# Third-stage operands split from the transposition's bank, weight preparation and activations re-ranked, six first weight loads issued by GpSimd: a fused chunk attention and two-stage mixture kernel

## The chip, the core and the metric

The kernel runs on one core of one Trainium2 chip. The metric is the device time of one execution in microseconds (us). The median of three executions of the kernel before is 812.74 us (812.33 to 813.37). The trace comes from another execution, recorded by the hardware profiler: it took 814.69 us, of which 812.9 us lie between the first and the last instruction (the span). What is worked out from the trace is compared with 814.69 and then taken over to the median, which is 1.95 us lower.

## The reference

Three stages follow each other; every one takes the result of the one before.

```
attention: per chunk of 32 queries, keys = 8 memory keys + 16 left + 32 own + 8 right (W = 64)
    a = exp(q k^T / sqrt(64) - max);  a = a / (sum(a) + 1e-9);  out = a @ v        (2 x 8 heads x 768 x 64)
x  = out as [1536 tokens, 512]
moe:   p = probs / (sum(probs) + 1e-9);  x = sum over 4 experts of p[e] * (relu(x @ w1[e]) @ w2[e])   (512 -> 1024 -> 512)
moe2:  h = x @ w_in;  g = h if h > 0 else exp(min(h, 0)) - 1;  out = g @ w_out       (512 -> 2048 -> 512)
```

All is computed to float32 accuracy. TensorE gets it by three products of two parts: a value is split into a rounded high part (a cast on ScalarE) and the rest (a subtraction on VectorE or GpSimd), and each product is high x high + low x high + high x low.

## The kernel before, in words

The 1536 tokens are two halves g = 0, 1 of 768, each six blocks of 128. The hidden layers are cut into units u of 512 hidden values: eight in the mixture (4 experts x 2), four in moe2 (u = 8 to 11). A step of the program is a unit and a half; the sequence is (0,0), (1,0), (1,1), (2,1), (2,0), ..., (7,0), (7,1), (0,1), (8,0), (8,1), ..., (11,1), 24 steps.

Each step has an "up" part and a "down" part. Up multiplies tokens by w1 or w_in with seven block products instead of eight (a Strassen form). Its token operands are seven matrices of 128 x 768 per half: three are blocks of x (B11, B21, B22, numbered 0, 1, 2) and four are sums and differences of blocks (T1, T2, T3, T4N, numbered 3 to 6). They are called xh (high) and xl (low) with half and number: xl1_5 is the low part of operand 5 of half 1. The weights' parts are uh and ul. One step's up is 84 matmuls of 128x384 (L570; L630 in the first step). Down multiplies the activated hidden values (hh, hl, four row groups f of 128, two token halves) by w2 or w_out (dh, dl): 72 matmuls of 128x512 (L664).

The helper `split_task` adds the two tasks of every split: ScalarE's cast (L249) and the subtraction (L245) on VectorE or GpSimd. `combine` builds the seven operands of a half from the transposed x, which lies in the SBUF buffer `area`: it needs subtractions of blocks for the T operands, then seven splits. Before the third stage x is the sum y of the second; `flip` transposes it, one block of 128 tokens at a time, into PSUM bank 6 or 7 (L709), and ScalarE copies the bank to `area` (L712). `activate` turns a product into hh and hl: for moe2 two ScalarE functions (L519, L520), one VectorE operation (L525), a cast to hh (L530) and a subtraction to hl.

`load_pair` loads a unit's w1 (two tiles rawp, 512 KB each), `prep_down` its w2 (four tiles rawd, 256 KB each), and both split them. `block_at` adds the attention of a block; its key, query and value loads (L759, L765) go out on SyncE's DMA queue, as the weight loads do. `convert` puts w_in and w_out, which come with 64-bit words, into float32 and stores them in DRAM for the third stage.

The order on every engine is set by a small planner in the program. Every task has an engine, an estimated duration and a rank; the planner repeatedly picks, for the engine that is free first, the ready task of the lowest rank, and emits it. RANK and BY are tables of such ranks and of engine choices. The emitted order is then fixed: an engine works through its own list and stands still when the next entry isn't ready.

Of the kernel before, what the change touches and what calls it, by code (L numbers as in the profile page):

```python
# [19 lines left out]
P = 128  # L20
# [39 lines left out]

RANK = {
# [117 lines left out]
def kernel(ctx, tc, att, w1, w2, w_in, w_out, probs, out):  # L179
# [90 lines left out]
    def split_blocks(u, j, i, rank, o, n, to=0, by=None):  # L270
# [14 lines left out]
    def prep_pair(u, j, rank, lead, by=None, plain=False):  # L285
        load_pair(u, j, rank - lead)
# [124 lines left out]
    def combine(g, rank, late, spare, parts, engs):  # L411


        base, rest = combiner(g, spare, parts, engs)
        base(rank, late)
        rest(late)

    def combiner(g, spare, parts, engs):
# [10 lines left out]
        def split(o, b, rank, name=None):  # L429
            for i, c in enumerate(cut):  # L430
                eng = pick(f"b{g}{o if name is None else name}{i}", "V") if parts > 1 or spare else "V"
                split_task(
                    rank,
                    2 * n,
                    b[0][:, :, c],
                    keys(b, c),
                    lambda c=c: xh[g][o][:, :, c],
                    ("xh", g, o, i) if parts > 1 else ("xh", g, o),
                    lambda c=c: xl[g][o][:, :, c],
                    ("xl", g, o, i) if parts > 1 else ("xl", g, o),  # L440
                    eng,
                )
            if parts > 1:
                for k in ("xh", "xl"):
                    join[k, g, o] = [(k, g, o, i) for i in range(parts)]
# [14 lines left out]
        def base(rank, late, plain=False):  # L460
            split(B11, blk(0), rank)
            split(B21, blk(2), rank)
            if plain:
                split(B12, blk(1), late, 7)
                split(B22, blk(3), late)

        def rest(late, plain=False):
            if spare:
                s0 = 2 * KT * TN
                t2 = area[:, s0 : s0 + 2 * TN].rearrange("p (k t) -> p k t", k=2), [grains(s0, TN), grains(s0 + TN, TN)]  # L470
                diff(engs[0], blk(0), blk(1), blk(0), late)
                diff(engs[1], t2, blk(3), blk(0), late)
                diff(engs[2], blk(1), blk(3), blk(1), late)
            else:
                t2 = blk(3)
                diff(engs[0], blk(0), blk(1), blk(0), late)
                split(B22, blk(3), late)
                diff(engs[1], blk(1), blk(3), blk(1), late)
                diff(engs[2], t2, blk(3), blk(0), late)
            diff(engs[3], blk(2), blk(2), t2, late)  # L480
            split(T2, t2, late)
            split(T3, blk(1), late + 1)
            split(T4N, blk(2), late + 3)
            split(T1, blk(0), late + 5)
            if spare and not plain:
                split(B22, blk(3), late + 7)

        return base, rest
# [65 lines left out]
    def up(u, g, rank):  # L554
# [3 lines left out]
        for n, (p, j) in enumerate([(p, j) for j in range(2) for p in ORDER] if apart else [(p, j) for p in ORDER for j in range(2)]):  # L558
# [20 lines left out]
            add("PE", 1.051, r, mm, [("uh", j, i), ("ul", j, i)] + xkeys(g, ib), kb)  # L579
# [36 lines left out]
    def plain(half, rank):  # L616

        for n, (q, f) in enumerate([(q, f) for f0 in (0, 2) for q in range(2) for f in (f0, f0 + 1)]):
# [19 lines left out]
            add("PE", 1.051, rank + n, mm, [("uh", j, i), ("ul", j, i)] + xkeys(0, ib), kb)  # L638
# [62 lines left out]
    def flip(g, tb, rank):  # L701
# [9 lines left out]
        add("PE", 0.49, rank, turn, [("y", g, tb)], [("b", b)])  # L711
# [288 lines left out]
```

## Time and profile before

| what | value |
|---|---|
| median of 3 executions | 812.74 us (812.33 to 813.37) |
| profiled execution | 814.69 us |
| its span | 812.9 us |
| mean granted TensorE clock | 0.998 of full speed |
| busy TensorE / weight load / VectorE / ScalarE / GpSimd | 799.4 / 722.0 / 517.9 / 421.2 / 295.9 us |
| moved by DMA | 72.13 MB, mean 89 GB/s |

A busy time is the sum over an engine's instructions, and its share is of the span. TensorE is busy for 799.4 us of 812.9, so 13.5 us of the span are left in which it does nothing. A row of a timeline gives the start in us, the duration in us, the engine, the line, what is written and read, and how many like instructions stand in a row; a bracket behind it is idle time of the engine before it and what ended that. Matmuls overlap in the pipeline, so what one costs is the distance from its start to the next start, not its duration.

### The profile page before, as it was taken

How to read it: one execution, taken by the hardware profiler on the slowest of the kernel's cores; microseconds unless marked ns; L12 is line 12 of the kernel's file. 1: busy time of each engine (PE TensorE's matmuls, PEld its weight loads, DVE VectorE, ACT ScalarE, POOL GpSimd, SP SyncE). 2: the span in 40 equal slices, each digit the busy share in tenths (PEclk: the TensorE clock that was granted, in tenths of full speed). 3: DMA queues.
4: the chain of work that ended last, by engine and by line, in shares of the span. 5: the costliest groups of instructions: out<-in, count | busy, mean ns of one | idle time of the engine just before them, and what ended most of it. 6: DMA issues, size and time to landing. Idle time of an engine off the chain costs nothing.

```text
span 812.9 us, 12177 instructions
## 1 busy us (share of the span) xinstructions
PE 799.4 (98%) x4684; PEld 722.0 (89%) x4684; DVE 517.9 (64%) x832; ACT 421.2 (52%) x857; POOL 295.9 (36%) x266
## 2 busy tenths in 40 slices
PE   7999999999999999999999999999999999999998
PEld 6888889989989989989989989899798898998997
DVE  5895557986965976965865734855535537538534
ACT  5976636625525425425425436457566555555642
POOL 2547275215215214324323325754216216206202
PEclk9999999999999999999999999999999999999999
DMA  8974112722411521511421300212003003000012
GB/s 307 341 248 165 33 46 84 220 91 72 166 67 59 194 79 40 204 56 66 156 78 65 130 1 1 85 44 78 1 1 104 0 1 93 11 1 0 35 45 79
DMA packets 27419, 72.13 MB, mean 89 GB/s; under 512 B 3168, under 2 KB 3424, under 8 KB 27360
## 3 DMA queue, kind: packets, MB, share of 16 engines
q1 hardware_dynamic: 27360, 71.34, 26.0%
q8 instruction: 37, 0.61, 0.3%
q14 instruction: 22, 0.18, 0.1%
HBM read 59.79 MB, written 11.53 MB: 88 GB/s over the span
## 4 chain that ended last, share of the span: by engine, by line
PE 86%; ACT 3%; issue 3%; DMA 2%; DVE 2%; POOL 2%; SPq 0%; POOLq 0%; ACTq 0%
PE bank L664 46%; PE bank L570 36%; DMA qk<-in_att_dram 2%; PE bank L630 1%; POOL area L245 1%; PE bank L862 1%; POOL hl L245 1%; DVE xl L245 1%; ACT abd L850 1%; PE bank L785 1%; ACT xh L249 1%; ACT e L813 0%; ACT hh L500 0%; ACT hh L530 0%; PE bank L842 0%
## 5 line engine op out<-in xcount | busy, mean ns | idle before, releaser
L664 PE MATMUL bank<-dh,hl 128*128 128x512 f32 x580 | 226.0, 390 | 2.0 <-DVE hl L245 2.0
L664 PE MATMUL bank<-dh,hh 128*128 128x512 f32 x580 | 226.6, 391 | 0.1
L664 PE MATMUL bank<-dl,hh 128*128 128x512 f32 x580 | 225.7, 389 | 0.0
L570 PE MATMUL bank<-xh,uh 128*128 128x384 f32 x644 | 218.2, 339 | 0.4 <-ACT p L582 0.4
L570 PE MATMUL bank<-xh,ul 128*128 128x384 f32 x644 | 216.8, 337 | 0.0
L570 PE MATMUL bank<-xl,uh 128*128 128x384 f32 x644 | 216.8, 337 | 0.0
L245 POOL TENSOR_TENSOR hl<-c,hh 128x384 fp32r<-128x384 f32 x63 | 71.8, 1147 | 216.1 <-ACT hh L530 214.8
L664 PEld LDWEIGHTS bank<-dh,hl 128*128 128x128 f32 x580 | 109.3, 188 | 25.5 <-DVE hl L245 2.4
L664 PEld LDWEIGHTS bank<-dh,hh 128*128 128x128 f32 x580 | 109.3, 188 | 21.9 <-ACT hh L500 0.5
L664 PEld LDWEIGHTS bank<-dl,hh 128*128 128x128 f32 x580 | 109.4, 189 | 21.3
L570 PEld LDWEIGHTS bank<-xh,uh 128*128 128x128 f32 x644 | 120.9, 188 | 1.9 <-ACT p L582 0.7
L570 PEld LDWEIGHTS bank<-xl,uh 128*128 128x128 f32 x644 | 120.9, 188 | 0.9
L570 PEld LDWEIGHTS bank<-xh,ul 128*128 128x128 f32 x644 | 120.9, 188 | 0.0
L302 POOL TENSOR_TENSOR rawp<-rawp 128x256 f32<-128x256 f32 x96 | 89.3, 943 | 16.0 <-DVE ul L245 10.5
L245 DVE TENSOR_TENSOR ul<-rawp,uh 128x512 fp32r<-128x512 f32 (+1 forms) x71 | 73.1, 1043 | 32.0 <-ACT uh L249 31.3
L690 DVE SCALAR_TENSOR_TENSOR y<-bank,pr,y 128x512 f32<-128x512 f32 x84 | 62.3, 747 | 48.5 <-PE bank L664 48.5
L245 POOL TENSOR_TENSOR hl<-area,hh 128x384 fp32r<-128x384 f32 x32 | 36.5, 1157 | 148.8 <-ACT hh L530 142.4
L249 ACT CAST uh<-rawp 128x512 fp32r<-128x512 f32 (+1 forms) x76 | 52.1, 686 | 68.9 <-POOL rawp L302 68.3
L377 ACT ACTIVATE area<-area 128x512 f32<-128x512 f32 x32 | 20.3, 634 | 86.9 <-DVE area L368 86.7
L245 POOL TENSOR_TENSOR dl<-rawd,dh 128x512 fp32r<-128x512 f32 x25 | 39.1, 1573 | 58.7 <-ACT dh L249 56.2
L525 DVE SCALAR_TENSOR_TENSOR area<-area,bank 128x384 f32<-128x384 f32 x32 | 17.6, 550 | 65.2 <-ACT area L520 65.2
L582 ACT COPY bank<-bank 128x384 f32<-128x384 f32 x46 | 21.2, 463 | 72.8 <-PE bank L570 72.8
(85 smaller groups left out, 962.7 us busy)
## 6 DMA issues: line engine op xcount, KB each, us to landing
rawp<-in_w_dram SPq DMA_DIRECT2D x18, 512.0 KB, 3.3
rawd<-in_w_dram SPq DMA_DIRECT2D x36, 256.0 KB, 3.6
qk<-in_att_dram SPq DMA_DIRECT2D x11, 768.0 KB, 6.9
area<-in_w_in_dram SPq DMA_DIRECT2D x16, 512.0 KB, 3.6
stash<-area SPq DMA_DIRECT2D x32, 256.0 KB, 2.2
area<-in_w_out_dram SPq DMA_DIRECT2D x16, 512.0 KB, 4.3
v<-in_att_dram SPq DMA_DIRECT2D x12, 512.0 KB, 5.3
rawp<-stash SPq DMA_DIRECT2D x16, 256.0 KB, 2.7
```

The lines of the kernel that those rows point to most:

```text
L245: e.tensor_tensor(out=dst, in0=a, in1=b, op=ALU.subtract)
L249: add("A", t_a(n), rank, lambda: A.copy(out=hi(), in_=src), rkeys, [hkey])
L302: lambda o=o, a=a, b=b, op=op: G.tensor_tensor(out=r[:, o], in0=r[:, a], in1=r[:, b], op=op),
L377: lambda: A.activation(out=t, in_=t, func=AF.Copy, scale=2.0**-20, bias=1.0),
L525: lambda: V.scalar_tensor_tensor(out=r, in0=r, scalar=-1.0, in1=v, op0=ALU.add, op1=ALU.max),
L570: PE.matmul(out=acc, lhsT=s[:, k], rhs=x[g][ib][:, k], start=(first and k == 0 and m == 0), stop=(k == 1 and m == 2), skip_group_check=True,)
L582: add("A", t_a(TN), r - 2, lambda: A.copy(out=dst, in_=acc), kb, kd)
L630: PE.matmul(out=acc, lhsT=s[:, k], rhs=x[0][ib][:, k], start=(q == 0 and k == 0 and m == 0), stop=(q == 1 and k == 1 and m == 2),)
L664: PE.matmul(out=po, lhsT=s[f][half][:, t0 : t0 + P], rhs=w[f][:, c], start=(q == 0 and i == 0), stop=(q == NF - 1 and i == 2),)
L690: lambda: V.scalar_tensor_tensor(out=yy(), in0=po, scalar=p, in1=yy(), op0=ALU.mult, op1=ALU.add),
L785: PE.matmul(out=s4[64 * cp : 64 * cp + 64, hp, ch], lhsT=qbd[:, hp, c], rhs=k[:, hp, c], start=True, stop=True,)
L850: (A.copy if by == "A" else V.tensor_copy)(out=abd[64 * ch : 64 * ch + 64, :, :, :, ch, :].rearrange("p h c i q -> p (h c i) q"), in_=tr[6 ...
```

## The change

Five things change.

1. `flip` adds, through the new `blocks_x`, the splits of the operands B11, B21 and B22 of the third stage directly from the transposition's bank, block by block: per half nine ScalarE casts and nine VectorE subtractions of 128x256. `combine` no longer splits these three operands from `area` for the third stage (three of 128x768 each before). Their splits have rank `fx` = -18.99 beside the transposition's own.
2. The rest of `combine` for the third stage (differences and T operands) is ranked `x0` = 74.72 (half 0) and `x1` = 51.82 (half 1) behind its step's rank, where both had 29.7; the four differences of half 1 are on "GGVV" (G is GpSimd, V VectorE) instead of "GGGG".
3. The weights' preparation of a unit's up part is ranked `pp` = 40.18 behind the step before it (14 before); that of the down part `pd` = -5.43 (+2 before), and its subtractions are on "VGVV" (VGVG before), which brings the fourth from GpSimd to VectorE. Down's matmuls are ranked 0.42 earlier, activations 2.67 later.
4. The six weight loads of the first step (rawp1, rawp0, rawd0 to rawd3) are issued from GpSimd and not from SyncE.
5. A table without users (MORE) is gone, and `combine` is one function where it was two. The matmuls are the same in number and kind.

```diff
 RANK = {
...
-    "pair1": 73.5, "pairs1": -8.67, "down1": 29.32, "c0t": 28.82,
+    "pair1": 73.5, "pairs1": -8.67, "down1": 29.32, "c0t": 28.82, "x0": 74.72, "x1": 51.82, "engx0": "VVGG",
+    "engx1": "GGVV", "pp": 40.18, "pd": -5.43, "engd": "VGVV", "dd": -0.42, "fx": -18.99, "ac": 2.67,
 }
...
-    def load_pair(u, j, rank):
+    def load_pair(u, j, rank, first=False):
         keys = [("rp", j, i) for i in range(4)]
         if u < NU1:
-            add("D", 1.46, rank, lambda: nc.sync.dma_start(out=rawp[j].rearrange("p b c -> p (b c)"), in_=w1[u, j]), (), keys)
+            q = nc.gpsimd if first else nc.sync
+            add("D", 1.46, rank, lambda: q.dma_start(out=rawp[j].rearrange("p b c -> p (b c)"), in_=w1[u, j]), (), keys)
...
-            lambda: nc.sync.dma_start(out=rawd[f], in_=stash[u, "d", f] if src is None else src),
+            lambda: (nc.gpsimd if by == "d" else nc.sync).dma_start(out=rawd[f], in_=stash[u, "d", f] if src is None else src),
...
+    def split_x(g, o, c, src, rkeys, rank, eng="V"):
+
+        i = None if c.stop - c.start == TN else c.start // P
+        split_task(
+            rank,
+            2 * (c.stop - c.start),
+            src,
+            rkeys,
+            lambda: xh[g][o][:, :, c],
+            xkeys("xh", g, o, i),
+            lambda: xl[g][o][:, :, c],
+            xkeys("xl", g, o, i),
+            eng,
+        )
+
+    def blocks_x(g, b, n, t0, rank):
+
+        v = bank[b].rearrange("p (k t) -> p k t", k=KT)
+        for q, o in enumerate(((B11, B21), (None, B22))[n]):
+            if o is not None:
+                split_x(g, o, slice(t0, t0 + P), v[:, 2 * q : 2 * q + 2], [("b", b)], rank)
...
-            activate(u, f, half, v, vkeys, r, ring["e"])
+            activate(u, f, half, v, vkeys, r + RANK["ac"], ring["e"])
...
         add("PE", 0.49, rank, turn, [("y", g, tb)], [("b", b)])
+        blocks_x(g, b, n, t0, rank + RANK["fx"])
         add("A", t_a(DM), rank, lambda: A.copy(out=xf[n][:, :, t0 : t0 + P], in_=ft), [("b", b)], keys)
...
-                    prep_pair(u, j, at(i - 1) + 14, 8)
+                    prep_pair(u, j, at(i - 1) + RANK["pp"], 8)
             for f in range(NF):
-                prep_down(u, f, RANK["down1"] if first else at(i) + 2, 8, "VGVG"[f], "e" if first else None)
+                prep_down(u, f, RANK["down1"] if first else at(i) + RANK["pd"], 8, RANK["engd"][f], "e" if first else None)
...
-                down(i, at(i) + 13.9)
+                down(i, at(i) + 13.9 + RANK["dd"])
...
-                combine(g, at(i) + 29.7, at(i) + 29.7, g == 0, 1, "VVGG" if g == 0 else "GGGG")
+                combine(g, at(i) + RANK[f"x{g}"], g == 0, 1, RANK[f"engx{g}"])
```

Three places show how the order on an engine moves. The first is VectorE in step (8,0), where half 0's first hidden values of moe2 are activated while half 1's operands are being built. In the names hl0_0 is the low part of row group 0, token half 0; c0 to c3 are scratch tiles; the number behind the last underscore is a buffer's. Before:

```order
L525 SCALAR_TENSOR_TENSOR area_144<-area_144,bank0_63 128x384
L591 TENSOR_TENSOR c2_142<-bank4_67,p7_0_138 128x384
L525 SCALAR_TENSOR_TENSOR area_144<-area_144,bank1_64 128x384
L591 TENSOR_TENSOR c3_143<-bank5_68,p7_1_139 128x384
L591 TENSOR_TENSOR c0_140<-bank2_65,u2_0_136 128x384
L245 TENSOR_TENSOR xl1_4_1306<-area_144,xh1_4_1299 128x768
L245 TENSOR_TENSOR xl1_5_1307<-area_144,xh1_5_1300 128x768
L245 TENSOR_TENSOR xl1_6_1308<-area_144,xh1_6_1301 128x768
L245 TENSOR_TENSOR xl1_3_1305<-area_144,xh1_3_1298 128x768
L245 TENSOR_TENSOR hl0_0_122<-area_144,hh0_0_114 128x384
L245 TENSOR_TENSOR hl1_0_124<-area_144,hh1_0_116 128x384
```

The same place on VectorE now:

```order
L529 SCALAR_TENSOR_TENSOR area_144<-area_144,bank0_63 128x384
L590 TENSOR_TENSOR c2_142<-bank4_67,p7_0_138 128x384
L243 TENSOR_TENSOR area_144<-area_144 128x768
L590 TENSOR_TENSOR c3_143<-bank5_68,p7_1_139 128x384
L243 TENSOR_TENSOR hl0_0_122<-area_144,hh0_0_114 128x384
L590 TENSOR_TENSOR c0_140<-bank2_65,u2_0_136 128x384
L529 SCALAR_TENSOR_TENSOR area_144<-area_144,bank1_64 128x384
L590 TENSOR_TENSOR c1_141<-bank3_66,u2_1_137 128x384
L529 SCALAR_TENSOR_TENSOR area_144<-area_144,c2_142 128x384
L243 TENSOR_TENSOR hl1_0_124<-area_144,hh1_0_116 128x384
```

The four splits of half 1's T operands (xl1_3 to xl1_6) moved behind the whole activation, and one of the differences (128x768) came from GpSimd into it.

The second is TensorE at the border of up and down in step (7,1). Before:

```order
L570 MATMUL bank3_66<-xh1_6_1301,ul1_0_99 128x384
L664 MATMUL bank0_63<-dh0_106,hh0_0_114 128x512
L664 MATMUL bank0_63<-dl0_110,hh0_0_114 128x512
L664 MATMUL bank0_63<-dh0_106,hl0_0_122 128x512
L664 MATMUL bank0_63<-dh1_107,hh1_0_116 128x512
L664 MATMUL bank0_63<-dl1_111,hh1_0_116 128x512
L664 MATMUL bank0_63<-dh1_107,hl1_0_124 128x512
L570 MATMUL bank4_67<-xh1_2_1297,uh0_1_91 128x384
```

And now:

```order
L569 MATMUL bank3_66<-xh1_6_1301,ul1_0_99 128x384
L569 MATMUL bank4_67<-xh1_2_1297,uh0_1_91 128x384
L569 MATMUL bank4_67<-xl1_2_1304,uh0_1_91 128x384
L569 MATMUL bank4_67<-xh1_2_1297,ul0_1_97 128x384
L569 MATMUL bank4_67<-xh1_2_1297,uh0_1_91 128x384
L569 MATMUL bank4_67<-xl1_2_1304,uh0_1_91 128x384
L569 MATMUL bank4_67<-xh1_2_1297,ul0_1_97 128x384
L569 MATMUL bank5_68<-xh1_2_1297,uh1_1_94 128x384
```

Six matmuls of down, which stood ahead of the last two groups of up, follow them now, as in the other steps of the mixture.

The third is GpSimd in the first step, while attention runs (e0 and e1 are the attention's weights, z0 and z1 their sums). Before:

```order
L245 TENSOR_TENSOR xl0_0_81<-area_144,xh0_0_74 128x2x128 x2
L245 TENSOR_TENSOR xl0_1_82<-area_144,xh0_1_75 128x2x128
L832 TENSOR_TENSOR e0_167<-e0_167,z1_173 128x512
L245 TENSOR_TENSOR ul1_2_101<-rawp1_89,uh1_2_95 128x256
L245 TENSOR_TENSOR ul0_0_96<-rawp0_88,uh0_0_90 128x768
L245 TENSOR_TENSOR ul0_2_98<-rawp0_88,uh0_2_92 128x256
L832 TENSOR_TENSOR e1_168<-e1_168,z0_172 128x512
L245 TENSOR_TENSOR xl0_3_84<-area_144,xh0_3_77 128x2x128
L245 TENSOR_TENSOR area_144<-area_144 128x2x128
L245 TENSOR_TENSOR xl0_4_85<-area_144,xh0_4_78 128x2x128
```

GpSimd now, a few rows longer (rawd3 follows eight rows on):

```order
L255 DMA rawp1_89<-in_w1_dram 128x1024
L243 TENSOR_TENSOR xl0_0_81<-area_144,xh0_0_74 128x2x128
L243 TENSOR_TENSOR xl0_1_82<-area_144,xh0_1_75 128x2x128
L832 TENSOR_TENSOR e0_167<-e0_167,z1_173 128x512
L255 DMA rawp0_88<-in_w1_dram 128x1024
L243 TENSOR_TENSOR ul1_2_101<-rawp1_89,uh1_2_95 128x256
L243 TENSOR_TENSOR ul0_0_96<-rawp0_88,uh0_0_90 128x768
L243 TENSOR_TENSOR ul0_2_98<-rawp0_88,uh0_2_92 128x256
L832 TENSOR_TENSOR e1_168<-e1_168,z0_172 128x512
L243 TENSOR_TENSOR xl0_3_84<-area_144,xh0_3_77 128x2x128
L243 TENSOR_TENSOR area_144<-area_144 128x2x128
L314 DMA rawd0_102<-in_w2_dram 128x512
```

The loads wait for nothing themselves, but each now stands behind GpSimd operations of the attention and of the first operands, which wait for other engines. The first xl0_0 stands just ahead of rawp1; rawd1 and rawd2 follow the next xl0_4.

## Rows read from the trace of the kernel before

**Rows 1.** The page: span, then busy time, share and instructions of each engine.

```profile
span 812.9 us, 12177 instructions
...
PE 799.4 (98%) x4684; PEld 722.0 (89%) x4684; DVE 517.9 (64%) x832; ACT 421.2 (52%) x857; POOL 295.9 (36%) x266
```

**Rows 2.** Waits of TensorE: line and releaser, us in total, times, longest.

```profile
PE bank L664 <- DVE hl L245: 2.0, 1, 2.0
```

**Rows 3.** Busy us of PE, PEld, DVE, ACT, POOL in stretches; granted clock, DMA share, GB/s.

```profile
20.00:30.00 10.00, 8.74 (x181) 7.72 (x182) 9.65 (x17) 8.83 (x23) 4.57 (x6) 1.00 0.99 367
...
150.00:160.00 10.00, 10.00 (x59) 10.00 (x58) 9.83 (x17) 5.14 (x13) 2.23 (x2) 1.00 0.87 253
...
570.00:580.00 10.00, 8.02 (x32) 6.45 (x31) 8.88 (x14) 6.62 (x15) 2.54 (x3) 0.83 0.01 2
```

**Rows 4.** TensorE's timeline in step (8,0), where down begins.

```profile
572.00 0.40 PE L664 MATMUL bank<-dl,hh 128*128 128x512 f32 x1
574.37 0.63 PE L664 MATMUL bank<-dh,hl 128*128 128x512 f32 x1 [1.98 <-DVE hl L245]
...
578.13 0.40 PE L664 MATMUL bank<-dh,hl 128*128 128x512 f32 x1
578.36 0.39 PE L664 MATMUL bank<-dh,hh 128*128 128x512 f32 x1
```

**Rows 5.** VectorE's timeline at the same place.

```profile
569.46 4.39 DVE L245 TENSOR_TENSOR xl<-area,xh 128x768 fp32r<-128x768 f32 x4
573.77 1.01 DVE L245 TENSOR_TENSOR hl<-area,hh 128x384 fp32r<-128x384 f32 x2
```

**Rows 6.** ScalarE's timeline at the same place.

```profile
567.78 0.50 ACT L530 CAST hh<-area 128x384 fp32r<-128x384 f32 x1
```

**Rows 7.** GpSimd's timeline at the same place.

```profile
562.20 8.23 POOL L245 TENSOR_TENSOR area<-area 128x768 f32<-128x768 f32 x4 [1.77 <-ACT area L712]
```

**Rows 8.** TensorE's timeline in step (7,1), where down begins.

```profile
508.74 0.39 PE L664 MATMUL bank<-dh,hl 128*128 128x512 f32 x1
...
510.29 0.39 PE L664 MATMUL bank<-dh,hh 128*128 128x512 f32 x1
```

**Rows 9.** SyncE's DMA queue: issues, with the time an issue takes.

```profile
15.46 0.43 SPq L256 DMA_DIRECT2D rawp<-in_w_dram  x1
```

**Rows 10.** Line L256 up to 110 us: the six rawp loads, issue to landing.

```profile
DMA to landing us min/median/max: 3.5/7.2/8.2
```

**Rows 11.** Line L315 up to 110 us: the twelve rawd loads, issue to landing.

```profile
DMA to landing us min/median/max: 2.7/5.1/7.1
```

**Rows 12.** GpSimd's timeline in the first step.

```profile
19.47 0.72 POOL L245 TENSOR_TENSOR xl<-area,xh 128x256 fp32r<-128x256 f32 x1 [2.22 <-ACT xh L249]
...
24.74 1.05 POOL L832 TENSOR_TENSOR e<-e,z 128x512 f32<-128x512 f32 x1
...
37.94 0.73 POOL L245 TENSOR_TENSOR xl<-area,xh 128x256 fp32r<-128x256 f32 x1 [2.94 <-ACT xh L249]
```

**Rows 13.** ScalarE's timeline in the first step.

```profile
23.65 0.83 ACT L249 CAST uh<-rawp 128x768 fp32r<-128x768 f32 x1
24.78 0.59 ACT L873 COPY area<-bank 128x512 f32<-128x512 f32 x1 [0.30 <-PE bank L862]
...
28.61 0.84 ACT L249 CAST uh<-rawp 128x768 fp32r<-128x768 f32 x1
29.89 0.59 ACT L873 COPY area<-bank 128x512 f32<-128x512 f32 x1 [0.44 <-PE bank L862]
...
31.43 1.75 ACT L813 ACTIVATE e<-bank,m 128x64 f32<-128x64 f32 x8 [0.65 <-DVE m L809]
...
39.90 1.13 ACT L249 CAST dh<-rawd 128x512 fp32r<-128x512 f32 x2
```

**Rows 14.** VectorE's timeline in the first step.

```profile
41.03 1.28 DVE L245 TENSOR_TENSOR dl<-rawd,dh 128x512 fp32r<-128x512 f32 x2
```

**Rows 15.** TensorE's timeline in the first step, down's first matmuls.

```profile
43.18 0.39 PE L664 MATMUL bank<-dl,hh 128*128 128x512 f32 x1
```

More of the change, by code (lines that the diff above doesn't have):

```diff
@@ L409, in convert, with xkeys, combine @@
         add("D", 0.73, rank, store, kt, [("st", u, k, c)])
[L411 to L418, printed above, removed]
+    def xkeys(k, g, o, i=None):
+        return [(k, g, o, n) for n in range(TN // P)] if i is None else [(k, g, o, i)]
+    def split_x(g, o, c, src, rkeys, rank, eng="V"):
[16 more added lines that the diff above has]
+                split_x(g, o, slice(t0, t0 + P), v[:, 2 * q : 2 * q + 2], [("b", b)], rank)
+    def combine(g, late, spare, parts, engs, first=False, stage="", rank=0):
         n = TN // parts
@@ L430, in split @@
             for i, c in enumerate(cut):
[L431 to L445, printed above, removed]
+                by = pick(f"b{g}{o if name is None else name}{i}", "V") if first else "V"
+                split_x(g, o, c, b[0][:, :, c], keys(b, c), rank, by)
         def diff(eng, o, a, b, rank):
@@ L458, in diff @@
                 )
-        def base(rank, late, plain=False):
+        if stage == "plain":
             split(B11, blk(0), rank)
             split(B21, blk(2), rank)
[L463 to L488, printed above, removed]
+            split(B12, blk(1), late, 7)
+            split(B22, blk(3), late)
+            return
+        if first and g:
+            split(B11, blk(0), late)
+            split(B21, blk(2), late)
+        if spare:
+            s0 = 2 * KT * TN
+            t2 = area[:, s0 : s0 + 2 * TN].rearrange("p (k t) -> p k t", k=2), [grains(s0, TN), grains(s0 + TN, TN)]
+            diff(engs[0], blk(0), blk(1), blk(0), late)
+            diff(engs[1], t2, blk(3), blk(0), late)
+            diff(engs[2], blk(1), blk(3), blk(1), late)
+        else:
+            t2 = blk(3)
+            diff(engs[0], blk(0), blk(1), blk(0), late)
+            diff(engs[1], blk(1), blk(3), blk(1), late)
+            diff(engs[2], t2, blk(3), blk(0), late)
+        diff(engs[3], blk(2), blk(2), t2, late)
+        split(T2, t2, late)
+        split(T3, blk(1), late + 1)
+        split(T4N, blk(2), late + 3)
+        split(T1, blk(0), late + 5)
+        if first and g:
+            split(B22, blk(3), late + 7)
     def scratch():
@@ L922 @@
         down(0, RANK["d00"], RANK["d01"])
-        rest(RANK["c0t"], True)
+        combine(0, RANK["c0t"], True, 3, RANK["eng0"], True)
         prep(1)
@@ L926 @@
             block_at(j, RANK["a1"] + RANK["a1s"] * (j - NB), RANK["lead"])
-        top = [(k, 1, o) for k in ("xh", "xl") for o in range(7)] + [("y", 1, tb) for tb in range(NB)]
+        top = [n for k in ("xh", "xl") for o in range(7) for n in xkeys(k, 1, o)] + [("y", 1, tb) for tb in range(NB)]
         add("N", 0, 50, switch, used, used + top)
-        combine(1, RANK["c1"], RANK["c1"], True, 1, RANK["eng1"])
+        combine(1, RANK["c1"], True, 1, RANK["eng1"], True)
         for i in range(len(conv)):
```

27 lines of the change are left out of this document (10 added, 17 removed).

## The prediction

> **What bounds the kernel now.** I read the page's busy times first: TensorE works 799.4 us of a span of 812.9 [rows 1], so whatever the change does to the other engines counts only where TensorE waits for them, and there are 13.5 us to gain at most. The list of TensorE's waits comes second: after the first stage one is long, 2.0 us of down's matmuls (L664) for a subtraction hl on VectorE, once [rows 2]. Third come the windows: between 570 and 580 us TensorE is busy 8.02 of 10 and the granted clock is 0.83, while 150 to 160 is full; in 20 to 30 it is busy 8.74, with the DMA engines at 0.99 [rows 3]. So two places matter: the first step, where attention, the operands and the weights come together, and the border of the second stage to the third.
>
> At that border the timelines say why. hl0_0, half 0's first low part in step (8,0), needs only hh0_0, and ScalarE has that at 567.78 + 0.50 = 568.3 [rows 6]. VectorE, however, stands at four subtractions of 128x768 (xl1_3 to xl1_6, half 1's T operands) from 569.46 for 4.39 us, and takes hl0_0 and hl1_0 at 573.77 [rows 5]. Half 1's operands aren't needed before step (8,1), about 15 us later. In their turn they stood there because GpSimd makes all four differences from 562.20 on in 8.23 us [rows 7].
>
> **The change part by part.**
>
> *The stall.* Matmuls of 128x512 follow each other at 0.23 us (578.13 to 578.36). The one at 574.37 would have started at 572.00 + 0.23 = 572.23, so 2.14 us are lost. From 574.37 to 578.13 lie nine steps: 3.76 us instead of 9 x 0.23 = 2.07, so 1.69 more [rows 4]. In this stretch the granted clock is 0.83 of full speed on the average, after an idle time of 1.98 us; before and behind it it is 1.00 [rows 3, 4]. Full speed is the 2.4 GHz level; the nine steps of 0.42 us in the mean have most of their time at the 1.2 GHz one. That goes with the stall. After the change the four T subtractions stand behind the whole activation. Ahead of hl0_0 are now one addition, one difference of 128x768 and one more addition; by [rows 5] a 128x768 is 4.39/4 = 1.1 us. With hh0_0 at about the same time, hl0_0 is ready near 570, over 2 us before 572.2. Gain 2.14 + 1.69 = 3.83.
>
> *What is late next there.* hl2_0 is: VectorE has a second difference of 128x768 ahead of it (1.1 us); by adding up its list I get 575.8 against a need at 575.9 in the schedule without the stall. The nearest row for being late is the wait of 2.0 itself.
>
> *The smaller gap.* In step (7,1) four steps from 508.74 take 1.55 us to 510.29, where 4 x 0.23 = 0.92 are due [rows 8]: 0.63 lost. Six matmuls of down stood ahead of the last up groups there; the new order is that of the other steps of the mixture, which show no such gap, and the subtractions of the third stage's operands, which crowd VectorE there, are ranked later. Gain 0.63, or nothing if the activation's cast is late for another reason. So the gains are up to 3.83 + 0.63 = 4.46.
>
> *Operands from the bank.* Nine casts and nine subtractions of 128x256 take the place of three and three of 128x768: the same elements, six more instruction starts on each engine and half. All stand beside full TensorE stretches on engines with idle time (VectorE 64%, ScalarE 52% [rows 1]): nothing, with the cover of [rows 3] for the worst case: in 150 to 160 VectorE is busy 9.83 of 10. One thing tightens: the bank is free for the next transposition only when the casts and subtractions have read it, not the copy alone. It costs nothing as long as VectorE isn't behind.
>
> *Weights later.* From step (2,1) on (about 150 us) the low parts of up's weights come behind dl and pieces of the conversion on a VectorE that is full there [rows 3]. Adding up its list, an estimate, I find the last of them ready about 0.1 us ahead of the matmul that reads it. The fourth dl brings VectorE 0.65 us a unit. Together with hl2_0 I take +0.5 for these tight places, bounded by 0 and by one such wait as is seen, 2.0 [rows 2].
>
> *The six loads on GpSimd.* On SyncE rawp1 is issued at 15.46 [rows 9] and lands 8.2 later [rows 10], at 23.66; ScalarE casts it at once, at 23.65. On GpSimd it follows the first xl0_0, whose end is 19.47 + 0.72 = 20.2. rawp0 follows e0, 24.74 + 1.05 = 25.8, and rawd1 the next xl0_4, 37.94 + 0.73 = 38.7 [rows 12]. No row shows a load by GpSimd. From both sides: as fast as the fastest SyncE load up to 110 us, 3.5 for rawp and 2.7 for rawd, or as slow as the slowest, 8.2 and 7.1 [rows 10, 11]. A value between: the fast one with its transfer doubled, since the stretch's 367 GB/s are already taken [rows 3] and a second queue gets perhaps half. 512 KB at 367 are 1.43 us, 256 KB 0.71: 4.9 and 3.4, an estimate. The slowest belong to a queue with several loads ahead of them, so I stay with it.
>
> What it costs, by ScalarE's list [rows 13], where the casts stand in unchanged order. rawp1 lands at 20.2 + 4.9 = 25.1 and not 23.65: 1.45 late, of which 0.30 is idle time behind it. rawp0 lands at 25.8 + 4.9 = 30.7, its cast stood at 28.61: 2.1 late, of which 0.44 + 0.65 idle: 1.0 remains, and the first delay is contained in it. rawd1 goes out at 38.7 + 1.0 and lands at 43.1; its cast was second of the pair at 39.90, so at 40.4: 2.7 late. Its dl ended at 41.03 + 1.28 = 42.3 [rows 14], and TensorE read it at 43.18 [rows 15]: 0.9 of slack, so 1.8 late in all. By the fast ends rawp1 lands in time, rawp0 within its idle time, rawd1 at 41.4, 1.0 late less 0.9: +0.1. By the slow ends rawp0 lands at 34.0, 5.4 - 1.1 = 4.3 late, and rawd1 at 38.7 + 4.3 + 7.1 = 50.1, 9.7 - 0.9 = 8.8 late. SyncE's queue gains: attention's loads no longer stand behind six weight loads. TensorE's waits name no such load in the list beyond a few tenths, so I count nothing for it.
>
> *What is written on GpSimd's loads points both ways.* The Trainium skill ("DMA: Bandwidth & Descriptors", section "Anatomy of one DMA — SWDGE (gpsimd) path") gives about 2.0 us plus bytes/436e3 for such a load, which would be 3.2 and 2.6 us and hardly any loss (near the +0.1 above). The same skill ("SBUF — State Buffer", the note on the "DVE blocks DMA" trap) warns that GpSimd cannot write its descriptors while VectorE holds the port they share. No run here shows either yet; VectorE is busy 9.65 of 10 in 20 to 30 [rows 3].
>
> **Sum.** -4.46 + 1.8 + 0.5 = -2.2. The profiled execution's 814.69 becomes 812.5; the median, 1.95 lower, 812.74 - 2.2 = 810.5.
>
> **The rivals.**
>
> (a) *Slower: GpSimd's loads are as slow as SyncE's slowest.* Place: first step, where nothing stands between a late weight and TensorE. With +8.8 the sum is -4.46 + 8.8 + 0.2 = +4.5, 817.2. It decides from 4.5 - 0.5 = 4.0 us of delay. For it: GpSimd's operations ahead of the issues, DMA engines that are full, VectorE nearly full, so that the descriptors may come late. Against: the issue itself waits for nothing, and a queue of its own has nothing ahead of it. The note on the trap in the Trainium skill's SBUF page would work in this direction.
>
> (b) *All gains, no loss.* -4.46 + 0.1 + 0.0 = -4.4, 808.4. For it: the quiet rows of 3.5 and 2.7. Against: the DMA share of 0.99.
>
> (c) *The stall comes back in another place.* hl2_0 or the weights at 150 us are late by as much as 2.0 and take the clock down with them, as at 574: the gain of 3.83 shrinks to about 2, and with 1.8 from the first step the time stays within 812 to 814, say 813. For it: margins of 0.1 us that I only added up. Against: VectorE's mean is 64%.
>
> (d) *The change doesn't free hl0_0*, since its cast is ranked later too, and ScalarE's casts of half 1 stand ahead of it: 812.74 + 1.8 + 0 - 0.6 = 813.9. Against: these casts moved behind as well.
>
> **How the numbers follow.** Forecast (-2.2) 0.38, (b) 0.16, (c) 0.19, (d) 0.07, (a) 0.20. A difference of 0.2% or 1.6 us is about what a measurement of this kernel can tell from none. Faster by more: most of the forecast (0.33) and (b), with a little of (c): 0.52. Within 0.2%: the rest of the forecast, most of (c) and (d): 0.27. Slower: (a) and the edge of (d): 0.21. The forecast's own range, with the loads between 0.1 and 4.3 us and the tight places between 0 and 2, is 808.5 to 813. For 8 in 10 it reaches to 807.8 below (all gains and a few tenths of SyncE's relief) and to 816.0 above, into (a).
>
> **What would show it.** Right: no wait on hl at the border of (8,0), steps of 0.23 there, a granted clock of 1.00 in 570 to 580; uh's first cast at about 25 and TensorE's busy time in 20 to 50 lower by about 1.8; the gap of step (7,1) gone. Wrong: casts of rawp later than 28 or of rawd1 later than 46; a new wait for ul at 150 or for hl2_0 behind 575; the chain of waits through GpSimd's loads.

## The result, and the profile after

The changed kernel takes 823.14 us (median of 4 executions, 821.61 to 825.64) against 813.04 us of the kernel before (a fourth execution has moved its median from 812.74): a ratio of 1.013, with an interval of 1.011 to 1.015. It is slower by some 10 us where 2.2 us less were forecast, and it lies beyond the slow end of the range, 816.0. The profiled execution took 821.99 us with a span of 819.5, 6.6 us more than before.

The page of the changed kernel, lines of [rows 1]:

```profile
span 819.5 us, 12207 instructions
...
PE 804.3 (98%) x4684; PEld 725.2 (88%) x4684; DVE 509.9 (62%) x860; ACT 423.1 (52%) x869; POOL 268.2 (33%) x256
```

TensorE runs the same 4684 matmuls, but is busy for 804.3 us in place of 799.4: some of them ran slower. TensorE's waits in the changed kernel, as in [rows 2] (left out are the wait for the idents at the start, attention's own, and two of about 0.4 us that the kernel before has too):

```profile
PE bank L629 <- ACT xh L247: 2.5, 2, 1.8
...
PE bank L629 <- POOL ul L243: 1.3, 1, 1.3
...
PE bank L663 <- ACT dh L247: 0.9, 1, 0.9
...
PE bank L663 <- DVE dl L243: 0.2, 1, 0.2
PE bank L629 <- ACT uh L247: 0.2, 1, 0.2
```

The wait of 2.0 us for hl is gone, and all the new ones are in the first step: L629 is its up part, L663 with dh and dl its down part. The windows say the same, read as [rows 3]:

```profile
20.00:30.00 10.00, 7.10 (x143) 6.08 (x140) 7.68 (x15) 6.54 (x17) 3.82 (x6) 1.00 0.88 310
30.00:40.00 10.00, 8.57 (x65) 7.52 (x64) 4.00 (x12) 6.16 (x22) 4.45 (x5) 0.83 0.64 254
40.00:50.00 10.00, 8.35 (x122) 6.87 (x120) 6.42 (x14) 6.36 (x14) 4.00 (x6) 1.00 0.58 196
50.00:60.00 10.00, 9.04 (x56) 7.39 (x57) 6.73 (x18) 4.79 (x11) 4.57 (x6) 0.66 0.71 233
...
580.00:590.00 10.00, 10.00 (x49) 8.63 (x48) 8.99 (x16) 9.32 (x21) 3.58 (x3) 1.00 0.01 2
```

The border of the stages has moved with everything behind the first step: down of step (8,0) now begins at 582.20, so its window is 580 to 590. It is full at a granted clock of 1.00: this half of the change works. Between 20 and 60 us TensorE idles, and the clock is 0.83 and 0.66 in two windows. GpSimd's timeline shows the loads going out, where [rows 12] had only the operations around them. The third row is work on rawp0, for which GpSimd stands still before it reaches the rawd loads:

```profile
19.44 0.70 POOL L255 DMA_DIRECT2D rawp<-in_w_dram  x1
...
25.31 0.59 POOL L255 DMA_DIRECT2D rawp<-in_w_dram  x1
...
35.55 2.50 POOL L243 TENSOR_TENSOR ul<-rawp,uh 128x768 fp32r<-128x768 f32 x2 [6.59 <-ACT uh L247]
...
40.89 0.59 POOL L314 DMA_DIRECT2D rawd<-in_w_dram  x1
...
43.90 1.09 POOL L314 DMA_DIRECT2D rawd<-in_w_dram  x2
```

ScalarE's timeline shows when they are there, as [rows 13]:

```profile
26.53 0.83 ACT L247 CAST uh<-rawp 128x768 fp32r<-128x768 f32 x1 [3.36 <-DMA rawp<-in_w_dram]
...
34.64 0.83 ACT L247 CAST uh<-rawp 128x768 fp32r<-128x768 f32 x1 [3.79 <-DMA rawp<-in_w_dram]
...
48.71 0.62 ACT L247 CAST dh<-rawd 128x512 fp32r<-128x512 f32 x1 [2.90 <-DMA rawd<-in_w_dram]
```

rawp1 comes 2.9 us later than before (23.65), rawp0 6.0 (28.61), rawd1 8.3 (about 40.4). The time from issue to landing of rawp0 alone is this line of its DMA's view:

```profile
DMA to landing us min/median/max: 9.3/9.3/9.3
```

In the kernel before, rawp0 went out on SyncE's queue ahead of attention's next loads (each qk is 768 KB):

```profile
21.93 0.43 SPq L256 DMA_DIRECT2D rawp<-in_w_dram  x1
...
25.19 1.33 SPq L759 DMA_DIRECT2D qk<-in_att_dram  x3
```

TensorE's timeline of the changed kernel in the first step's down part:

```profile
47.58 0.39 PE L663 MATMUL bank<-dh,hh 128*128 128x512 f32 x1
...
49.38 0.49 PE L663 MATMUL bank<-dh,hh 128*128 128x512 f32 x1 [0.94 <-ACT dh L247]
50.10 0.50 PE L663 MATMUL bank<-dl,hh 128*128 128x512 f32 x1 [0.23 <-DVE dl L243]
...
51.58 0.69 PE L629 MATMUL bank<-xh,uh 128*128 128x384 f32 x1 [0.74 <-ACT xh L247]
...
56.07 0.63 PE L663 MATMUL bank<-dh,hh 128*128 128x512 f32 x1
...
57.48 1.38 PE L785 MATMUL bank<-qk,qbd 128*64 128x64 f32 x32
...
63.52 0.39 PE L663 MATMUL bank<-dh,hh 128*128 128x512 f32 x1
```

The four rows of dh,hh are the first matmuls on rawd0, rawd1, rawd2 and rawd3. After waits of 0.94, 0.23 and 0.74 us the twelve matmuls of 128x384 from 51.58 to 56.07 take 0.37 us each.

### The profile page after: what moved, and what is told of

Same layout as the page of the kernel before. It is cut to its first block, busy times and chain, and to the rows that moved or that the text cites. A ratio compares the mean times of both kernels' runs of the same rounds, so it can differ in the third digit from the quotient of the medians.

```text
span 819.5 us, 12207 instructions
## 1 busy us (share of the span) xinstructions
PE 804.3 (98%) x4684; PEld 725.2 (88%) x4684; DVE 509.9 (62%) x860; ACT 423.1 (52%) x869; POOL 268.2 (33%) x256
## 4 chain that ended last, share of the span: by engine, by line
PE 92%; DMA 4%; ACT 2%; DVE 1%; POOL 1%; issue 0%; SPq 0%; ACTq 0%; DVEq 0%
PE bank L663 48%; PE bank L569 41%; DMA qk<-in_att_dram 2%; PE bank L629 1%; DMA rawp<-in_w_dram 1%; DMA rawd<-in_w_dram 1%; PE bank L708 1%; PE bank L785 1%; PE bank L862 1%; ACT e L813 0%; POOL xl L243 0%; PE bank L842 0%; POOL e L832 0%; DVE z L820 0%; ACT qbd L773 0%
## 5 line engine op out<-in xcount | busy, mean ns | idle before, releaser
L663 PE MATMUL bank<-dh,hh 128*128 128x512 f32 x580 | 226.1, 390 | 0.9 <-ACT dh L247 0.9
L663 PE MATMUL bank<-dl,hh 128*128 128x512 f32 x580 | 225.4, 389 | 0.2 <-DVE dl L243 0.2
L663 PE MATMUL bank<-dh,hl 128*128 128x512 f32 x580 | 225.4, 389 | 0.0
L663 PEld LDWEIGHTS bank<-dh,hl 128*128 128x128 f32 x580 | 109.0, 188 | 23.0 <-DVE hl L509 0.2
L663 PEld LDWEIGHTS bank<-dh,hh 128*128 128x128 f32 x580 | 109.0, 188 | 22.5 <-ACT dh L247 1.4
L663 PEld LDWEIGHTS bank<-dl,hh 128*128 128x128 f32 x580 | 109.1, 188 | 21.8 <-DVE dl L243 0.5
L301 POOL TENSOR_TENSOR rawp<-rawp 128x256 f32<-128x256 f32 x96 | 86.2, 910 | 20.6 <-DVE ul L243 14.4
L689 DVE SCALAR_TENSOR_TENSOR y<-bank,pr,y 128x512 f32<-128x512 f32 x84 | 62.6, 746 | 43.1 <-PE bank L663 42.9
L243 DVE TENSOR_TENSOR ul<-rawp,uh 128x512 fp32r<-128x512 f32 (+1 forms) x71 | 67.7, 969 | 30.5 <-ACT uh L247 30.4
L529 DVE SCALAR_TENSOR_TENSOR area<-area,bank 128x384 f32<-128x384 f32 x32 | 17.6, 549 | 68.6 <-ACT area L524 68.6
L243 POOL TENSOR_TENSOR dl<-rawd,dh 128x512 fp32r<-128x512 f32 x14 | 22.3, 1592 | 66.6 <-ACT dh L247 66.6
```

The lines of the kernel that those rows point to most:

```text
L243: e.tensor_tensor(out=dst, in0=a, in1=b, op=ALU.subtract)
L301: lambda o=o, a=a, b=b, op=op: G.tensor_tensor(out=r[:, o], in0=r[:, a], in1=r[:, b], op=op),
L529: lambda: V.scalar_tensor_tensor(out=r, in0=r, scalar=-1.0, in1=v, op0=ALU.add, op1=ALU.max),
L663: PE.matmul(out=po, lhsT=s[f][half][:, t0 : t0 + P], rhs=w[f][:, c], start=(q == 0 and i == 0), stop=(q == NF - 1 and i == 2),)
L689: lambda: V.scalar_tensor_tensor(out=yy(), in0=po, scalar=p, in1=yy(), op0=ALU.mult, op1=ALU.add),
```

## The experiments

**All six loads back on SyncE.** Nothing else is undone.

```diff
-            q = nc.gpsimd if first else nc.sync
+            q = nc.sync
...
-            lambda: (nc.gpsimd if by == "d" else nc.sync).dma_start(out=rawd[f], ...
+            lambda: nc.sync.dma_start(out=rawd[f], ...
```

> The changed kernel with its six first weight loads back on SyncE's queue; every other instruction and order as changed. Theory A (the whole loss is the first step's weights landing late, the third-stage part works): the changed kernel's span was 819.5 against 812.9, and its waits at 508 and 574 us are gone (4.5 us), so 812.9 - 4.5 = 808.4 of span and a median near 808.5, ratio to the kernel before 0.993 to 0.997, the first 60 us as in the kernel before. Rival B (the loss comes from the planner's new order or from the splits out of the bank): still above 816.

810.37 us (809.54 to 810.79), ratio 0.995 (0.9937 to 0.9963), span 808.7: theory A as expected. TensorE's timeline at the same four places:

```profile
42.31 0.39 PE L663 MATMUL bank<-dh,hh 128*128 128x512 f32 x1
...
43.01 0.39 PE L663 MATMUL bank<-dh,hh 128*128 128x512 f32 x1
...
45.78 0.39 PE L663 MATMUL bank<-dh,hh 128*128 128x512 f32 x1
...
52.41 0.39 PE L663 MATMUL bank<-dh,hh 128*128 128x512 f32 x1
```

At the last of them the changed kernel is 63.52 - 52.41 = 11.1 us late; the spans differ by 819.5 - 808.7 = 10.8. So the whole difference is made by then. The kernel before has its fourth dh at 52.36, like this version, so the rest of the program is worth 808.7 - 812.9 = -4.2 us of span. (By the medians the two versions differ by 12.8 us; the changed kernel's profiled execution is one of its two shorter ones.)

**The six loads on GpSimd in the kernel before.** The same two lines as in the change, put into that kernel alone.

> The kernel before with only the six first weight loads moved to GpSimd. Theory A: the loss alone, without the gain: 11 us in the profile's first 60 us, so a median of 822 to 827 (ratio 1.012 to 1.018), and the waits at 508 and 574 us still there. Rival B: 811 to 815.

825.05 us (818.52 to 826.96), ratio 1.0117 (1.0083 to 1.0152); the wait for hl is there with 2.0 us. The loads alone make a kernel slower that has nothing else of the change; the median is as expected, the ratio at the lower edge of it.

**Only rawd, and only rawp, on GpSimd.** Each undoes one of the two lines of the first experiment's diff.

> The changed kernel with only the four rawd loads on GpSimd, the two rawp loads back on SyncE. Theory A1 (both kinds cost, rawp more): GpSimd's list isn't delayed now, so rawd1 goes out near 39 and lands near 43.5, 2 to 3 us later than TensorE wants it: 810.5 to 812. Rival A2 (it is rawp alone): 808 to 809.5. Rival A3 (rawd alone): 818 or more.

816.13 us (815.04 to 818.29), ratio 1.0024 (1.0013 to 1.0035): more than expected.

> The changed kernel with only the two rawp loads on GpSimd, the four rawd loads back on SyncE. Theory A1: TensorE's first L663 stood 5.3 us later in the changed kernel than before, all of it behind rawp: 808.5 + 5 to 6 = 813.5 to 815. Rival A2 (rawp alone carries all): 819 or more. Rival A3 (rawd alone): 808 to 809.5.

815.63 us (813.73 to 818.54), ratio 1.0024 (1.0011 to 1.0037): a little more than expected, with the first L663 at 47.34, as in the changed kernel. Against 0.995, each kind costs about 0.74%, 6 us, most of the 1.8% that both cost together: A1, both kinds, but rawd no less than rawp. TensorE with rawd alone there:

```profile
41.62 0.39 PE L663 MATMUL bank<-dh,hh 128*128 128x512 f32 x1
...
44.09 0.51 PE L663 MATMUL bank<-dh,hh 128*128 128x512 f32 x1 [1.61 <-ACT dh L247]
44.82 0.50 PE L663 MATMUL bank<-dl,hh 128*128 128x512 f32 x1 [0.22 <-DVE dl L243]
...
46.13 0.69 PE L629 MATMUL bank<-xh,uh 128*128 128x384 f32 x1 [0.59 <-ACT xh L247]
...
50.63 0.63 PE L663 MATMUL bank<-dh,hh 128*128 128x512 f32 x1
```

The first row is even earlier than with all loads on SyncE (42.31). The three waits sum to 2.4 us, but at the last row TensorE is 50.63 - 41.62 - (45.78 - 42.31) = 5.5 us behind. Most of the difference is the clock: from 46.13 to 50.63 twelve matmuls take 4.50 us, where the same twelve take 45.78 - 43.70 = 2.1 at full speed with all loads on SyncE. My expectation had counted the waits alone.

**rawp0 alone on GpSimd.**

```diff
-            q = nc.gpsimd if first else nc.sync
+            q = nc.gpsimd if first and j == 0 else nc.sync
```

> The changed kernel with only rawp0 on GpSimd, rawp1 and the four rawd loads on SyncE. If rawp1's delay is contained in rawp0's, as the forecast had it: as late as with both rawp loads there, TensorE's first L663 near 47, ratio 1.001 to 1.004. If both delays add up: first L663 near 45, ratio 0.997 to 1.000.

817.43 us (816.62 to 819.3), ratio 1.0049 (1.0031 to 1.0066), L663 at 50.25. The delays don't add up; but the single load costs more than the two rawp loads together, which neither case of the expectation had. TensorE's timeline and its windows say why:

```profile
36.02 0.44 PE L629 MATMUL bank<-xh,uh 128*128 128x384 f32 x1 [4.08 <-ACT uh L247]
...
37.90 0.69 PE L629 MATMUL bank<-xh,ul 128*128 128x384 f32 x1 [1.15 <-POOL ul L243]
```

```profile
30.00:40.00 10.00, 4.77 (x21) 4.01 (x20) 1.74 (x6) 4.84 (x15) 3.96 (x4) 0.82 0.81 317
40.00:50.00 10.00, 9.63 (x126) 8.83 (x126) 6.64 (x15) 7.00 (x16) 3.00 (x5) 0.84 0.24 69
```

rawp0 took 9.6 us to land. With rawp1 in time TensorE ran into the missing rawp0 sooner and waited 4.08 + 1.15 us in two pieces, and the clock is low in both windows. With both rawp loads late the wait for ul ended 0.7 us sooner, at 37.20. The other 2.2 of the 2.9 us at L663 are the place of the low clock: here the matmuls behind 37.90 start 0.32 us apart and more until 43.1. There the low stretch was over by 33.8, ahead of the wait for ul, where TensorE would have had to wait anyway.

**The loads on GpSimd, but earlier in its list.** The planner emits them behind chosen GpSimd tasks (a hook in the loop that emits; all other lists unchanged).

```diff
+EARLY = {4: (1,), 5: (0,), 11: (2, 3, 4), 19: (5,)}
...
-            tasks[n][3]()
+            if n not in done:
+                tasks[n][3]()
+            if e == "G":
+                seen += 1
+                for i in EARLY.get(seen, ()):
+                    tasks[self.loads[i]][3]()
+                    done.add(self.loads[i])
```

> The changed kernel, its six loads still on GpSimd but standing earlier in GpSimd's list, close to the times at which SyncE issues them (rawp1 behind e1 near 16.5, rawp0 behind the first xl0_0 near 20, rawd0 to rawd2 behind ul0_2 near 32, rawd3 near 44); all other engines' lists as changed. Theory L (what costs is the late issue, behind GpSimd's own operations): back to the level of the version with all loads on SyncE, ratio 0.994 to 0.998, TensorE's first L663 near 42.5. Rival Q (GpSimd's loads themselves are slow, whenever they are issued): rawp0 still takes 9 us to land and not 5.5, so 2 us or more remain at the first L663 and the ratio is 1.000 or more.

813.07 us (811.62 to 814.17), ratio 0.9988 (0.9977 to 0.9998). Issued at 16.4 and 19.4, rawp1 and rawp0 were cast at

```profile
24.48 0.83 ACT L258 CAST uh<-rawp 128x768 fp32r<-128x768 f32 x1 [1.33 <-DMA rawp<-in_w_dram]
...
28.94 0.84 ACT L258 CAST uh<-rawp 128x768 fp32r<-128x768 f32 x1
```

and the first L663 stands at 43.72. Most comes back (1.013 to 0.9988, where 0.995 would be all of it), so the late issue is the larger part. It misses the range of theory L by a little: 0.4% remains. Rival Q's ratio of 1.000 isn't reached either. rawp0 took 7.9 us, neither 5.5 nor 9, but landed at 27.3, as SyncE's did with all loads there (issued at 22.00, 5.3 us). What remains is mostly the issuing itself. GpSimd's timeline, and a wait of TensorE:

```profile
32.34 1.67 POOL L329 DMA_DIRECT2D rawd<-in_w_dram  x3
34.01 1.06 POOL L847 TENSOR_TENSOR e<-e,z 128x512 f32<-128x512 f32 x1
```

```profile
PE bank L857 <- POOL e L847: 1.3, 2, 1.0
```

Three issues in a row hold GpSimd for 1.67 us and push attention's e behind them to 35.07; with all loads on SyncE the same operation starts at 32.08 and TensorE doesn't wait there. That wait of 1.0 us is most of the 43.72 - 42.31 = 1.4 us by which the first L663 is late. At the fourth dh it is still 53.83 - 52.41 = 1.4, of 2.0 us between the spans (810.7 and 808.7).

**The loads on ScalarE.**

```diff
-            q = nc.gpsimd if first else nc.sync
+            q = nc.scalar if first else nc.sync
...
-            lambda: (nc.gpsimd if by == "d" else nc.sync).dma_start(
+            lambda: (nc.scalar if by == "d" else nc.sync).dma_start(
```

> The changed kernel with the six first loads issued from ScalarE's list, a hardware queue like SyncE's, at the places that the planner's order gives them there: rawp1 near 21, rawp0 behind the cast of rawp1, rawd1 and rawd2 near 40. Theory L (a load that stands in the list of a working engine goes out late and then shares the DMA engines with attention's loads, whoever issues it): as slow as with GpSimd, ratio 1.006 or more, uh0's cast at 33 or later. Rival Q (GpSimd's software queue is what is slow): nearly the level of SyncE, 0.994 to 1.000.

816.87 us, widely spread (813.57 with a mean granted clock of 1.000 to 822.47 with 0.994), ratio 1.0057 (1.0032 to 1.0081). ScalarE's timeline:

```profile
24.52 0.33 ACTq L255 DMA_DIRECT2D rawp<-in_w_dram  x1
...
31.60 0.83 ACT L247 CAST uh<-rawp 128x768 fp32r<-128x768 f32 x1 [2.77 <-DMA rawp<-in_w_dram]
```

A hardware queue in a working engine's list is slow too: rawp0 goes out 24.5 and lands 7.1 us later. That is against rival Q. But rawp0 is there sooner than from GpSimd, and sooner than theory L said (31.60, not 33).

**A load by GpSimd in a quiet stretch.**

```diff
-            q = nc.gpsimd if first else nc.sync
+            q = nc.gpsimd if u == 2 else nc.sync
```

> All six first loads on SyncE; the two rawp loads of unit 2, which go out beyond 65 us where the DMA engines have little to do, on GpSimd. A measurement of one load by GpSimd by itself: SyncE's took 3.5 us from issue to landing in the quiet stretch. Rival Q (descriptors written by GpSimd cost time of their own): 5 us or more. Theory L: 3.5 to 4. The time itself should stay at the level of the version with the loads on SyncE (808 to 812).

One execution, 812.21 us, just above what was expected. The first of the two went out at 69.91; its DMA's view:

```profile
DMA to landing us min/median/max: 3.9/3.9/3.9
```

The other, issued at 81.10 and not at 77.00 as on SyncE, took 4.0. SyncE's fastest was 3.5 [rows 10], and the same two loads took 4.7 and 6.7 from SyncE in the version with all loads there. The stretch is quieter, not empty: in the 4 us that each load was on its way the DMA engines were busy 0.67 and 0.64 of the time,

```profile
70.00:74.00 4.00, 4.00 (x47) 3.35 (x46) 2.49 (x1) 3.71 (x7) 3.98 (x4) 1.00 0.67 204
81.00:85.00 4.00, 4.00 (x77) 3.47 (x76) 3.34 (x9) 3.65 (x8) 0.69 (x2) 1.00 0.64 206
```

where the changed kernel has 0.96 to 1.02 in its first step from 27 to 35 us. So the queue by itself costs a few tenths here, not 4 us.

**The third stage, part by part,** all with the loads on SyncE. First the old ranks of the combination:

```diff
-    ... "x0": 74.72, "x1": 51.82, "engx0": "VVGG",
-    "engx1": "GGVV", ...
+    ... "x0": 29.7, "x1": 29.7, "engx0": "VVGG",
+    "engx1": "GGGG", ...
```

> Loads on SyncE, operands from the bank, but the third stage's combination at its old ranks (29.7 for both halves, half 1's differences on GpSimd): VectorE has half 1's T subtractions ahead of hl0_0 again. Theory R (the ranks free hl0_0): the wait at the border of the stages is back with 2 us and a low clock behind it, ratio 0.998 to 1.001. Rival S (the splits out of the bank free VectorE early enough by themselves): no wait, ratio as with the new ranks, 0.994 to 0.996.

816.5 us (815.93 to 819.04), ratio 1.004 (1.0027 to 1.0054). TensorE's waits there:

```profile
PE bank L663 <- ACT hh L534: 2.8, 1, 2.8
PE bank L569 <- DVE c L590: 1.6, 2, 1.0
```

A wait at the border is back, and longer than in the kernel before: theory R. But it is for hh and not for hl: VectorE has three T subtractions from 571.15 on for 3.58 us ahead of the activation's own operation (L529, at 575.13), so that ScalarE's cast waits as well. And the low clock that was expected behind it is not there in the profiled execution: it took 815.93 us, the fastest of the seven, and its window 570 to 580 has 1.00 (the other six have a mean granted clock of 0.996 to 0.998). That it is worse than before wasn't expected; which of the other ranks makes it so was not tried. Then the operands from `area` again (`blocks_x` not called, their splits at rank 29.7):

```diff
-        blocks_x(g, b, n, t0, rank + RANK["fx"])
...
-        if first and g:
-            split(B11, blk(0), late)
-            split(B21, blk(2), late)
+        if not first or g:
+            split(B11, blk(0), rank if not first else late)
+            split(B21, blk(2), rank if not first else late)
```

> Loads on SyncE, new ranks, but B11, B21 and B22 of the third stage split from area as before (rank 29.7, three casts and three subtractions of 128x768 a half). Theory R: the gain stays, ratio 0.993 to 0.997. Rival S: the wait for hl at the border is back, or one for xl of the next step, ratio 0.998 or more.

810.71 us (809.93 to 811.13), ratio 0.9954 (0.9939 to 0.9969): the operands from the bank are worth nothing that can be measured. Then the weights' and activations' ranks as before:

```diff
-    ... "pp": 40.18, "pd": -5.43, "engd": "VGVV", "dd": -0.42, ... "ac": 2.67,
+    ... "pp": 14, "pd": 2, "engd": "VGVG", "dd": 0, ... "ac": 0,
```

> Loads on SyncE, operands from the bank and the third stage's combination at its new ranks, but the weights' preparation, down's matmuls and the activations ranked as before (14, +2, VGVG, 0, 0). Theory R (the combination's ranks alone free hl0_0): ratio 0.993 to 0.997, no wait for hl at the border. Rival T (the weights' and activations' ranks are needed too): the border's wait or the gap in step (7,1) is back, 0.998 or more.

810.97 us (809.26 to 812.03), ratio 0.9965 (0.9951 to 0.9978), no wait for hl. And last the kernel before with one line changed:

```diff
-                combine(g, at(i) + 29.7, at(i) + 29.7, g == 0, 1, "VVGG" if g == 0 else "GGGG")
+                combine(g, at(i) + 29.7, at(i) + (74.72, 51.82)[g], g == 0, 1, "VVGG" if g == 0 else "GGVV")
```

> The kernel before with one thing changed: the differences and T operands of the third stage ranked 74.72 and 51.82 behind their step in place of 29.7, half 1's differences on GGVV. Loads on SyncE, operands from area, all other ranks as before. Theory R (these ranks alone are the gain): no wait at the border of (8,0), ratio 0.993 to 0.997. Rival T (other parts are needed): 0.998 or more.

810.42 us (809.33 to 812.24), ratio 0.9958 (0.9944 to 0.9972). Its window at the border:

```profile
570.00:580.00 10.00, 10.00 (x49) 8.55 (x48) 9.02 (x16) 9.36 (x21) 3.55 (x3) 1.00 0.01 2
```

This line is the whole gain of the change; the windows 500 to 510 and 510 to 520, with the border of step (7,1), are full here too. It holds two ranks and the engines of half 1's differences; which of them does it was not tried. It and the changed kernel with its loads on SyncE are both faster than both kernels compared, and not to be told apart (0.9958 and 0.995).

## Why the prediction was wrong

**The gains were right.** 4.46 us were forecast for the stall, the low clock behind it and the gap in step (7,1). With the loads on SyncE the span is 4.2 us shorter, the windows 500 to 510 and 570 to 580 are full at clock 1.00, and VectorE's hl0_0 is done near 568.7, where I had said near 570:

```profile
568.17 0.55 DVE L243 TENSOR_TENSOR hl<-area,hh 128x384 fp32r<-128x384 f32 x1
```

Their cause was right too: the order of the T operands, shown by one line alone. One thing was overlooked. The 1.69 us for the low clock are not lost in every execution: of the 70 of the kernel before that were measured beside the experiments, 40 have a mean granted clock of 1.000 and 30 one of 0.998, with means of 813.1 and 814.7 us. The trace that I read was of the second kind, and the window behind the stall is the only one in it below 1.00.

**The tight places cost nothing.** The +0.5 for the weights at 150 us and for hl2_0 has no wait to show for it. Nor has the bank's longer reading.

**The step that failed is the six loads, mis-sized: +1.8 forecast, 11 measured.** The place, the order and the direction of their effect were as written, and rival (a), which is this mechanism, came true; but it was given 0.20 and priced at 817.2. Two of the recorded signs of being wrong are there: casts of rawp later than 28 and of rawd1 later than 46. Three things in the +1.8 were too small.

- *The landing.* I chose 4.9 us for rawp, the quiet load with its transfer doubled, and took SyncE's slowest, 8.2, for the upper end. rawp1 took 7.1; rawp0 took 9.3, beyond that end (8.5 to 9.6 in the three other runs that issue it from GpSimd at 25.5 to 25.9). A row that I had shows what I missed: SyncE's queue issues three loads of 768 KB from 25.19 on. On SyncE rawp0 went out at 21.93, ahead of them, and took 5.5; from GpSimd it goes out at 25.3, beside them. That it shares the engines with them is argued from the issue times and from the DMA share of 0.96 to 1.02 between 27 and 35 us; the runs show that a load of this size by the same queue takes 3.9 in a quieter stretch, and rawp0 7.1 from ScalarE's hardware queue at 24.5. What makes the 2 us between 7.1 and 9.3, the queue or the 0.8 us of later issue, stays open.
- *The issue moves with its own delay.* rawd1 was to go out at 38.7 + 1.0; it went at 43.9, because GpSimd's list had waited 6.59 us for uh0's cast in the meantime (2.26 in the kernel before). With rawp on SyncE it went at 38.0, near the 38.7 of [rows 12]. A load in a working engine's list is late by what that engine's other work is late.
- *The clock.* I charged the low clock to the stall at 574, but not to the waits that the late loads bring. From 51.58 to 57.48 the changed kernel takes 5.9 us for twelve matmuls of 128x384 and three of 128x512, 12 x 0.17 + 3 x 0.23 = 2.7 at full speed: about 3.2 us more, behind waits of 1.9 in all. The granted clock of 50 to 60 is 0.66: much of it at 1.2 GHz.

Put together: of the 11.1 us at the fourth dh, 47.58 - 42.31 = 5.3 were there at the first, behind rawp0; 5.0 more came by 56.07 (1.9 of waits, most of the rest clock), and 0.8 by 63.52. By the slow ends of the forecast rawp0 would have been cast at 34.0 and rawd1 at 50.1; they were cast at 34.64 and 48.71, and at the second dh TensorE was 49.38 - 43.01 = 6.4 us late, within the 8.8 of rival (a). What took the time beyond (a) is what came after that: one more wait and the low clock.

On GpSimd's loads, the formula of the Trainium skill ("DMA: Bandwidth & Descriptors", section "Anatomy of one DMA — SWDGE (gpsimd) path") gives 3.2 us for 512 KB, an estimate by that page. The run with the quieter stretch measured 3.9 and 4.0, and with attention's loads in flight it was 6.2 to 9.6; the measurement decides. No run here shows the trap that the Trainium skill ("SBUF — State Buffer", section "SBUF: two separate sides", the note on the "DVE blocks DMA" trap) warns of, that GpSimd can be locked out of writing a load's descriptors by VectorE. The load issued at 81.10 landed in 4.0 us with VectorE busy for 1.98 of the 2 us around its issue,

```profile
80.00:82.00 2.00, 2.00 (x14) 1.74 (x13) 1.98 (x4) 0.71 (x2) 1.58 (x2) 1.00 0.86 326
```

but whether those operations hold the port isn't shown. In the changed kernel VectorE stands idle for 2 us from 25.39 on, right behind the issue of rawp0,

```profile
27.39 0.96 DVE L243 TENSOR_TENSOR ul<-rawp,uh 128x768 fp32r<-128x768 f32 x1 [2.00 <-ACT uh L247]
```

and rawp0 still took 9.3, so waiting for VectorE isn't what made it slow.

## What to carry to other kernels

Before moving a load to another engine's queue, write down three times: when that engine's list reaches it, what else the DMA engines carry from then on, and when its data is wanted; a queue of its own doesn't help a load that stands behind compute. The issues take time too, from the work that stands behind them in that list. A wait of TensorE can cost more than its length: allow for the low-clock stretch that the trace shows behind a wait of like size (behind 2.0 us [rows 4] and behind three waits of 1.9 us in all there was one; behind the 2.8 us of the run with the old ranks there was none in the profiled execution). Where a fault is one wait, look for the one line that removes it (here one with two ranks), and try it by itself before anything is bundled with it.

## What the runs showed of the hardware

A load issued from GpSimd holds that engine for 0.54 to 0.72 us; ScalarE's issues took 0.33 to 0.39. Three in a row, 1.67 us, made TensorE wait 1.0 us for the operation behind them. Loads of 512 KB landed in 3.9 and 4.0 us from GpSimd where the DMA engines were busy 0.67 and 0.64 of the time, and in 3.5 at best from SyncE in the kernel before. What a low-clock stretch costs depends on where it falls: in the run with rawp0 alone it lay behind the wait for ul and the first L663 stood at 50.25; with both rawp loads on GpSimd it lay ahead of that wait, and the first L663 stood at 47.34.
